# Attention on TensorE in one piece per unit, a shorter bias table, one scalar transfer, and the first query tiles of both batches first

## The chip, the cores and the metric

The kernel runs on one core of a Trainium2 chip. The metric is device time in microseconds (us) of one execution, as the median of several; less is better. PE is TensorE (PEld its weight loads), DVE is VectorE, ACT is ScalarE, POOL is GpSimd, SP is SyncE, which here only issues DMAs.

## The reference, cut to what matters

```
scores = scale * q @ k^T                        # B=2, H=8, S=768, D=64, float32
keep = (pos_k < n_global) | (0 <= rel < n_local)     # 8 global keys, 96 local ones
dist = where(is_global & ~is_local, n_local, abs(rel))
scores = where(keep, scores - slope[h] * dist, -1e9)
a = softmax(scores); attn = a @ v               # as x: 1536 tokens x 512
x = ((x @ w_a) * (x @ w_b)) @ w_out             # d_ff = 1536
out = ((x @ w1) * (x @ w2)) @ w3 @ w_out2       # d_ff = 1024
```

## The kernel before

The work is cut into attention and two gated products stages. A query tile is 128 tokens of one batch (6 tiles for each of 2 batches), and a **unit** is four heads of a query tile: 24 units. A unit sees 232 keys (8 global, 96 before the tile, 128 own); in the first tile of a batch it sees only its own 128, and such a unit is called short. A unit takes these steps: scores (L558, four matmuls into banks 0 and 1), bias and row maximum (L533, DVE, from the table `tabs`), exponential (L537, ACT), sum plus 1e-9 and reciprocal (L579, L580, DVE), scaling (L542, POOL), transposes (L602, into banks 2 and 3), their copies to SBUF (L611 by ACT, L613 by DVE), values (L620, into bank 4), and two parts `xh` (L637, ACT) and `xl` (L638, DVE) of the result, which the products read.

The products are float32 in three float32r matmuls each (L188, L189, L190: high by high, high by low, low by high), 128x512 apiece, over three chunks of 512 tokens; 2352 such product matmuls stand in the program. Their weights come as float64 words in 1 MB transfers (L447) and pass through L455 to L465 on DVE, POOL and ACT (four DVE instructions a piece) into a `slot`. The first chunk needs four query tiles, that is eight units, and the weights `w_a` and `w_b` of group 0.

What order the engines work in is fixed beforehand. The class `Plan` lists operations as strands that each name an engine, a planned duration and the time when they are ready; it always takes the operation that could start first (a lower rank breaks ties), and the program is written in that order for every engine. So a strand's rank, its planned cost and how many operations it hands over together set the order. In `attention` each unit is a strand of its own: two score operations, and in `half(u)` two transposes operations and two values operations, each free to stand between products. A unit may begin when fewer than four are under way. The products are another strand of higher rank, and they fill PE where no attention is ready.

At the start, two DMAs on ACT's queue (L153, L154) bring the two int64 scalars; DVE turns them into floats (L159 to L164), sets a flag for a fallback that these inputs do not take (L175 to L180), and makes the bias table from two iotas in eight instructions (L198 to L201, L420 to L423); ACT and POOL scale it per head (L427, L429). The table's room is in `pT0`, `pT1` and `qk1`, so `qk1` can be loaded only after L427 and L429. SP issues all other DMAs in one queue.

Of the kernel before, what the change touches and what calls it, by code (L numbers as in the profile page):

```python
# [8 lines left out]
F32 = mybir.dt.float32  # L9
# [8 lines left out]
FMAX = 3.0e38  # L18

# [87 lines left out]
def attention_moe_moe_kernel(  # L107
# [4 lines left out]
    n_global: bass.AP,  # L112
    n_local: bass.AP,
# [45 lines left out]
    nc.vector.tensor_copy(wf, words)  # L159
    lo_w = wf.rearrange("p (n w) -> p n w", w=2)[:, :, 0]  # L160
    hi_w = wf.rearrange("p (n w) -> p n w", w=2)[:, :, 1]
    nc.vector.tensor_scalar(neg[:, 0:2], lo_w, 0.0, None, ALU.is_lt)
    nc.vector.tensor_tensor(neg[:, 2:4], neg[:, 0:2], hi_w, ALU.add)
    nc.vector.scalar_tensor_tensor(nval, neg[:, 2:4], 4294967296.0, lo_w, ALU.mult, ALU.add)  # L164
# [3 lines left out]

    ftmp = const.tile([P, 4], F32, tag="ftmp", name="ftmp")
    flag = const.tile([P, 1], I32, tag="flag", name="flag")  # L170

    const.tile([P, 40], F32, tag="gap", name="gap")
    xh = const.tile([P, KD, NT], F32R, tag="xh", name="xh")
    xl = const.tile([P, KD, NT], F32R, tag="xl", name="xl")
    nc.vector.tensor_scalar(ftmp[:, 0:1], ng, float(NG_MAX), None, ALU.is_gt)  # L175
    nc.vector.tensor_scalar(ftmp[:, 1:2], nl, 1.0, None, ALU.is_lt)
    nc.vector.tensor_scalar(ftmp[:, 2:3], nl, float(NPREV + 1), None, ALU.is_gt)
    nc.vector.tensor_tensor(ftmp[:, 3:4], ftmp[:, 0:1], ftmp[:, 1:2], ALU.max)
    nc.vector.tensor_tensor(ftmp[:, 0:1], ftmp[:, 2:3], ftmp[:, 3:4], ALU.max)
    nc.vector.tensor_copy(flag, ftmp[:, 0:1])  # L180
# [199 lines left out]
    D_MM = lambda n: 0.016 + 0.000417 * n  # L380
# [3 lines left out]
    with ExitStack() as fast:  # L384
# [32 lines left out]
        keep = jj  # L417
        masks(loc, keep, rel, jj)

        nc.vector.scalar_tensor_tensor(rel, rel, nl, loc, ALU.subtract, ALU.mult)  # L420
        nc.vector.scalar_tensor_tensor(rel, rel, nl, keep, ALU.add, ALU.mult)
        nc.vector.tensor_scalar(keep, keep, MASKED / slopes[-1], -MASKED / slopes[-1], ALU.mult, ALU.add)
        nc.vector.tensor_tensor(table, keep, rel, ALU.subtract)  # L423

        for h in range(H):
            if h < 5:
                nc.scalar.activation(tabs[:, h, :], table, AF.Copy, scale=8.0 * slopes[h])  # L427
            else:
                nc.gpsimd.tensor_scalar(tabs[:, h, :], table, 8.0 * slopes[h], 1.0, ALU.mult, ALU.mult)  # L429
        T0 = 10.5  # L430
        pl.free |= {"DVE": T0, "ACT": T0 + 2.5, "POOL": T0 + 2.0, "PE": 5.0}
        qkb.free[1] = T0 + 1.0

# [70 lines left out]

        xr = {}
        att = {"began": 0, "done": 0, "end": 0.0}
        obank = Ring([bank[4]])
        tbank = Ring([bank[2], bank[3]])
        sbank = Ring([(bank[0], bank[1])])
        tiles = {}  # L510

        def load(b, t):
            i, r = yield from qkb.get()
            j, r2 = yield from vvb.get()
            x, y = qkb.tiles[i], vvb.tiles[j]
            if t == 0:

                def fn():
                    nc.sync.dma_start(x[:, :, 0:P], qk[b, t, :, :, 0:P])
                    nc.sync.dma_start(x[:, :, P + KB:], qk[b, t, :, :, P + KB:])  # L520
                tq = yield op("DMA", 2.0, r, fn)
                tv = yield op("DMA", 0.9, r2, lambda: nc.sync.dma_start(y[:, 0, :], vv[b, t, :, 0, :]))
            else:
                tq = yield op("DMA", 2.4, r, lambda: nc.sync.dma_start(x, qk[b, t]))
                tv = yield op("DMA", 1.7, r2, lambda: nc.sync.dma_start(y, vv[b, t]))
            tiles[b, t] = i, j, tq + 2.2, tv + 2.2

        def head(rank, st, m, h, sS, ei, s, t, c0, res):

            n = KW - c0  # L530
            e = eb.tiles[ei][:, c0:KW]
            nmx, sm = st[:, m:m + 1], st[:, 4 + m:5 + m]
            a = yield op("DVE", 0.21 + 0.00104 * n, s, lambda: nc.vector.tensor_tensor_reduce(  # L533
                out=e, in0=sS, in1=tabs[:, h, 0:P] if t == 0 else tabs[:, h, P:TW],
                scale=-0.125, scalar=FMAX, op0=ALU.add, op1=ALU.min, accum_out=nmx))
            res["ttr"].append(a + LAT)
            a = yield op("ACT", D_ACT(n) + 0.28, a + LAT, lambda: nc.scalar.activation(  # L537
                e, e, AF.Exp, bias=nmx, scale=-1.0, accum_out=sm))
            res["exp"].append(a + LAT)

        def scaled(e, rs, r, res, u):
            res["e", u].append((yield op("POOL", 0.56, r, lambda: nc.gpsimd.tensor_scalar(  # L542
                e, e, rs, 1.0, ALU.mult, ALU.mult))) + LAT)

        def attention(num, b, t, g):

            yield lambda: 0.0 if att["began"] == num and (b, t) in tiles and num - att["done"] < 4 else None
            i, jv, tq, tv = tiles[b, t]
            x, y = qkb.tiles[i], vvb.tiles[jv]
            c0 = KB if t == 0 else 0  # L550
            sk, r = yield from sbank.get()
            sS = [bk.rearrange("p (u k) -> p u k", u=2)[:, :, 0:KW] for bk in [z[:, 0:2 * KW] for z in sbank.tiles[sk]]]

            def scores(u):
                p = 2 * g + u
                for j in range(2):
                    rr = slice(64 * j, 64 * j + 64)
                    nc.tensor.matmul(sS[j][:, u, c0:KW], x[rr, p, 0:P], x[rr, p, P + c0:P + KW], start=True, stop=True)  # L558

            s = []  # L560
            for u in range(2):
                s.append((yield op("PE", 0.32, max(tq, r), lambda u=u: scores(u))) + PELAT)
            att["began"] += 1
            k, r = yield from stb.get()
            st = stb.tiles[k]
            res = {"ttr": [], "exp": [], ("e", 0): [], ("e", 1): []}
            es = []
            for u in range(2):
                for j in range(2):
                    m = 2 * u + j  # L570
                    ei, r2 = yield from eb.get()
                    es.append(ei)
                    pl.spawn(head(num, st, m, 4 * g + m, sS[j][:, u, c0:KW], ei, max(s[u], r, r2), t, c0, res), 10 + 0.1 * num)
            sbank.free[sk] = yield lambda: max(res["ttr"]) if len(res["ttr"]) == 4 else None
# [402 lines left out]
```

## Time and profile before

| | |
|---|---|
| median of 3 runs | 650.99 us (649.75 to 652.82) |
| the profiled execution | 650.21 us |
| its span, first to last instruction | 648.3 us |
| PE busy in the span | 95% |
| DVE, ACT, POOL busy | 61%, 39%, 17% |
| the two scalar DMAs are issued | at 0.74 and 1.15 us |
| weights A and B of group 0 are issued | at 2.78 and 3.25 us |
| first product starts | at 60.15 us |

A row of the timeline gives start, duration, engine, line and operation; rows that repeat are merged with their count, and a wait ahead of a row stands in brackets with what ended it. PE's matmuls are pipelined: a row's duration overlaps the next one's, so what a matmul takes from the engine is the distance from one start to the next. A wait's releaser is inferred, and an engine that is named may have been done long before.

### The profile page before, as it was taken

Reading aid. Unit: us, or ns where it says so; the run is one execution under the profiler, and the core shown is the slowest. Engines: PE = TensorE matmul, PEld = TensorE weight load, DVE = VectorE, ACT = ScalarE, POOL = GpSimd, SP = SyncE. Lnnn points to the kernel's source line nnn. Section 1 sums busy time; section 2 is a strip of 40 time slices with the busy share of each in tenths; the row PEclk is TensorE's granted clock in tenths of the full one; section 3 lists DMA queues with packets and bytes.
Section 4 is the critical chain, followed back from the end, with each engine's and each line's share of the span. In section 5 each row is a group of like instructions: output and inputs, shape, how many; then the busy total and the mean of one; then the engine's idle time right before and its main releaser. Section 6 shows DMA issues by size and latency. Waiting matters only on the chain.

```text
span 648.3 us, 8069 instructions
## 1 busy us (share of the span) xinstructions
PE 617.2 (95%) x3072; PEld 496.1 (77%) x3072; DVE 394.4 (61%) x694; ACT 250.5 (39%) x486; POOL 108.9 (17%) x149
## 2 busy tenths in 40 slices
PE   1778999999999999999999999999999999999996
PEld 1445777777888888888888888888888888888884
DVE  5789765556366997766878654981376266323333
ACT  3767666554244434324343223542452133111110
POOL 3548423323022111101101100120021010000000
PEclk9989999999999999999999999999999999999999
DMA  7528222340033333303333000420240030000012
GB/s 251 195 104 312 63 79 108 128 163 1 1 130 129 131 129 130 130 1 130 129 131 115 16 0 1 161 99 1 73 174 13 1 130 2 1 0 1 32 66 102
DMA packets 12815, 57.79 MB, mean 89 GB/s; under 512 B 1504, under 2 KB 3552, under 8 KB 7904
## 3 DMA queue, kind: packets, MB, share of 16 engines
q1 hardware_dynamic: 12480, 57.19, 24.8%
q8 instruction: 26, 0.43, 0.3%
q14 instruction: 21, 0.17, 0.1%
q10 hardware_dynamic: 288, 0.00, 0.0%
HBM read 54.04 MB, written 3.15 MB: 88 GB/s over the span
## 4 chain that ended last, share of the span: by engine, by line
PE 93%; DVE 4%; DMA 1%; ACT 1%; issue 1%; POOL 0%; ACTq 0%; POOLq 0%; DVEq 0%; SPq 0%
PE bank L188 28%; PE bank L190 28%; PE bank L189 27%; PE bank L558 3%; PE bank L620 3%; PE bank L602 3%; DMA words<-in_n_local_dram 1%; DVE e L533 1%; DMA qk<-in_qk_dram 1%; DVE raw L460 1%; DVE pT L613 1%; ACT tabs L427 0%; DVE xl L638 0%; DVE acc L705 0%; DVE raw L458 0%
## 5 line engine op out<-in xcount | busy, mean ns | idle before, releaser
L188 PE MATMUL bank<-xh,slot 128*128 128x512 f32 x480 | 190.1, 396 | 0.0
L190 PE MATMUL bank<-xh,slot 128*128 128x512 f32 x480 | 187.0, 390 | 0.0
L189 PE MATMUL bank<-xl,slot 128*128 128x512 f32 x480 | 186.9, 389 | 0.0
L456 POOL TENSOR_SCALAR raw<-raw 128x1024 f32<-128x1024 f32 x38 | 54.0, 1425 | 337.9 <-DMA raw<-in_moe_w_dram 179.6
L705 DVE TENSOR_TENSOR acc<-acc,bank 128x512 f32<-128x512 f32 x96 | 65.7, 684 | 71.5 <-PE bank L190 71.3
L188 PEld LDWEIGHTS bank<-xh,slot 128*128 128x128 f32 x480 | 90.1, 188 | 21.4 <-issue 3.6
L190 PEld LDWEIGHTS bank<-xh,slot 128*128 128x128 f32 x480 | 90.1, 188 | 18.9
L189 PEld LDWEIGHTS bank<-xl,slot 128*128 128x128 f32 x480 | 90.2, 188 | 17.6
L668 ACT ACTIVATE gh<-gt 128x512 fp32r<-128x512 f32 x60 | 37.7, 629 | 112.4 <-DVE gt L664 112.4
L664 DVE TENSOR_TENSOR gt<-gt,bank 128x512 f32<-128x512 f32 x60 | 41.1, 685 | 64.6 <-PE bank L190 64.3
L661 ACT ACTIVATE gt<-bank 128x512 f32<-128x512 f32 x60 | 35.8, 597 | 87.8 <-PE bank L190 87.6
L542 POOL TENSOR_SCALAR e<-e,st 128x232 f32<-128x232 f32 (+1 forms) x96 | 51.6, 556 | 76.8 <-DVE st L580 37.9
L188 PE MATMUL bank<-gh,slot 128*128 128x512 f32 x144 | 56.9, 395 | 0.0
L189 PE MATMUL bank<-gl,slot 128*128 128x512 f32 x144 | 56.1, 390 | 0.0
L190 PE MATMUL bank<-gh,slot 128*128 128x512 f32 x144 | 56.1, 390 | 0.0
L457 ACT ACTIVATE raw<-raw 128x1024 f32<-128x1024 f32 x38 | 43.7, 1153 | 28.8 <-POOL raw L456 28.7
L458 DVE SCALAR_TENSOR_TENSOR raw<-raw 128x1024 int32<-128x1024 int32 x38 | 47.2, 1243 | 10.1 <-ACT raw L457 9.6
L537 ACT ACTIVATE e<-e,st 128x232 f32<-128x232 f32 (+1 forms) x96 | 44.6, 466 | 15.3 <-DVE st L533 14.8
L460 DVE SCALAR_TENSOR_TENSOR raw<-raw 128x1024 int32<-128x1024 int32 x38 | 49.4, 1301 | 0.5
L669 DVE TENSOR_TENSOR gl<-gt,gh 128x512 fp32r<-128x512 f32 x60 | 44.7, 746 | 4.7 <-ACT gh L668 4.5
L558 PE MATMUL bank<-qk 64*128 64x232 f32 (+1 forms) x192 | 27.6, 403 | 16.0 <-DMA qk<-in_qk_dram 10.9
L533 DVE CUSTOM_DVE_ANT_0 e<-bank,tabs 128x232 f32<-128x232 f32 (+1 forms) x96 | 32.7, 375 | 16.3 <-PE bank L558 15.2
(68 smaller groups left out, 735.0 us busy)
## 6 DMA issues: line engine op xcount, KB each, us to landing
raw<-in_moe_w_dram SPq DMA_DIRECT2D x16, 1024.0 KB, 4.8
raw<-in_moe_w_out_dram SPq DMA_DIRECT2D x10, 1024.0 KB, 5.1
qk<-in_qk_dram SPq DMA_DIRECT2D x10, 720.0 KB, 5.1
raw<-in_moe_w_a_dram SPq DMA_DIRECT2D x6, 1024.0 KB, 5.6
raw<-in_moe_w_b_dram SPq DMA_DIRECT2D x6, 1024.0 KB, 6.4
vv<-in_vv_dram SPq DMA_DIRECT2D x10, 512.0 KB, 3.6
out_dram<-acc SPq DMA_DIRECT2D x12, 256.0 KB, 2.0
qk<-in_qk_dram SPq DMA_DIRECT2D x4, 256.0 KB, 5.8
```

The source lines that it names most:

```text
L188: nc.tensor.matmul(po, sh, mh, start=first, stop=False)
L189: nc.tensor.matmul(po, sh, ml, start=False, stop=False)
L190: nc.tensor.matmul(po, sl, mh, start=False, stop=last)
L456: a = yield op("POOL", 1.2, t, lambda: nc.gpsimd.tensor_scalar(tf, tf, F64_MAX, -F64_MAX, ALU.min, ALU.max))
L457: a = yield op("ACT", D_ACT(1024), a + LAT, lambda: nc.scalar.activation(tf, tf, AF.Copy, scale=2.0 ** -112))
L458: c = yield op("DVE", 1.25, max(a, c) + LAT, lambda: nc.vector.scalar_tensor_tensor(low, top, 3, low, ALU.logical_shift_left, ALU.bitwise_or))
L460: t = yield op("DVE", 1.25, c + LAT, lambda: nc.vector.scalar_tensor_tensor(low, top, -0x80000000, low, ALU.bitwise_and, ALU.bitwise_or))
L537: a = yield op("ACT", D_ACT(n) + 0.28, a + LAT, lambda: nc.scalar.activation(e, e, AF.Exp, bias=nmx, scale=-1.0, accum_out=sm))
L542: res["e", u].append((yield op("POOL", 0.56, r, lambda: nc.gpsimd.tensor_scalar(e, e, rs, 1.0, ALU.mult, ALU.mult))) + LAT)
L558: nc.tensor.matmul(sS[j][:, u, c0:KW], x[rr, p, 0:P], x[rr, p, P + c0:P + KW], start=True, stop=True)
L669: a = yield op("DVE", D_DVE(CH), a + LAT, lambda: nc.vector.tensor_tensor(gl, gt, gh.bitcast(F32), ALU.subtract))
L705: u = yield op("DVE", D_DVE(CH), max(t + PELAT, accr[c, m]), lambda: nc.vector.tensor_tensor(a(), a(), po, ALU.add))
```

## The change

It does five things. The two scalars come as one array `n_words` that is laid out for 128 partitions, in one DMA. The table is made in six DVE instructions, three of them ahead of the scalars, in the room of the accumulators instead of `qk1`; five heads' tables are scaled by ACT, three by POOL as before; the flag's instructions become a strand of low rank. The query tiles go in the order (batch 0, batch 1) for tile 0, then for tile 1 and so on, so that the four short units come first; their q and k are loaded by pairs of heads. `load` is split in two strands, for q with k and for v. And PE's attention work becomes one strand: a piece holds the values of unit i-1, the transposes of unit i and the scores of unit i+2; from the ninth on it is one operation that waits for everything it needs. Planned costs of scores, transposes, values and products are changed too. Nothing of the arithmetic of the products changes.

```diff
-    nc.scalar.dma_start(words[:, 0:2], n_global.bitcast(I32).partition_broadcast(P))
-    nc.scalar.dma_start(words[:, 2:4], n_local.bitcast(I32).partition_broadcast(P))
+    nc.scalar.dma_start(words, n_words)
...
-    D_MM = lambda n: 0.016 + 0.000417 * n
+    D_MM = lambda n: 0.227 * n / 512
...
-        rel, jj, loc = [ptb.tiles[i][:, 0:TW] for i in range(2)] + [qkb.tiles[1].rearrange("p a b -> p (a b)")[:, 0:TW]]
-        table = qkb.tiles[1].rearrange("p a b -> p (a b)")[:, TW:2 * TW]
+        rel, relq, jj, near, dist = [a.rearrange("p m f -> p (m f)")[:, i * TW:(i + 1) * TW]
+                                     for a in accs for i in range(4)][:5]
...
-        masks(loc, keep, rel, jj)
-        nc.vector.scalar_tensor_tensor(rel, rel, nl, loc, ALU.subtract, ALU.mult)
-        nc.vector.scalar_tensor_tensor(rel, rel, nl, keep, ALU.add, ALU.mult)
-        nc.vector.tensor_scalar(keep, keep, MASKED / slopes[-1], -MASKED / slopes[-1], ALU.mult, ALU.add)
-        nc.vector.tensor_tensor(table, keep, rel, ALU.subtract)
+        nc.vector.tensor_scalar(near, rel, 0.0, 2.0 ** 20, ALU.is_lt, ALU.mult)
+        nc.vector.tensor_tensor(rel, rel, near, ALU.max)
+        nc.vector.tensor_scalar(relq, rel, 1.0 / FAR, None, ALU.mult)
+        read_words()
+        nc.vector.tensor_scalar(nlq, nl, 1.0 / FAR, None, ALU.mult)
+        nc.vector.scalar_tensor_tensor(near, rel, nl, relq, ALU.is_ge, ALU.add)
+        nc.vector.tensor_scalar(dist, jj, ng, nlq, ALU.is_ge, ALU.add)
+        nc.vector.tensor_tensor(dist, dist, near, ALU.min)
...
+        order = [(b, t) for t in range(NQ) for b in range(B)]
...
+        def load_qk(n, b, t):
...
             if t == 0:
...
+                for g in range(2):
+                    pp = slice(2 * g, 2 * g + 2)
+                    tq = yield op("DMA", 1.0, r, lambda pp=pp: nc.sync.dma_start(x[:, pp, KB:KB + 2 * P], qk[b, t, :, pp, KB:KB + 2 * P]))
...
+        def scores(num):
...
+            for u in range(2):
+                for j in range(2):
+                    rr = slice(64 * j, 64 * j + 64)
+                    nc.tensor.matmul(sS[j][:, u, 0:w], x[rr, 2 * g + u, KW:KW + P], x[rr, 2 * g + u, KW - w:KW], start=True, stop=True)
+        def transposes(num):
...
+            for m in range(4):
+                for c, (k0, _) in enumerate(blocks):
+                    i = (m % 2) * nb + c
+                    nc.tensor.transpose(pts[m // 2][:, i * P:(i + 1) * P], eb.tiles[ev["e", num][1][m]][:, k0:k0 + P], ident)
...
+            def part(what, num):
...
+                if what == "S":
+                    def r():
+                        if ("q", num) not in ev or (num and ("ttr", num - 1) not in ev):
+                            return None
...
+                    return r, 0.3 + 0.34 * nb, lambda: scores(num), then
...
+                    return r, 0.1 + 0.87 * nb, lambda: transposes(num), then
...
+                return r, 0.2 + 0.54 * nb, lambda: values(num), then
+            for i in range(-2, NU + 1):
+                ps = [part(w, n) for w, n in (("V", i - 1), ("T", i), ("S", i + 2)) if 0 <= n < NU]
+                whole = i > 8
+                for k in range(1 if whole else len(ps)):
+                    now = ps if whole else ps[k:k + 1]
...
+                    t = yield op("PE", sum(x[1] for x in now), t, fn)
...
-            for g in range(2):
-                pl.spawn(attention(2 * n + g, b, t, g), 8 + 0.1 * n)
+        pl.spawn(attention(), 8)
```

How the instructions move, at three places. **PE where attention stands among the products** (`bank_97` and `bank_98` before, `bank_87` and `bank_88` now, are product banks). Before:

```order
L188 MATMUL bank_97<-xh,slot_100 128x512
L189 MATMUL bank_97<-xl,slot_100 128x512
L190 MATMUL bank_97<-xh,slot_100 128x512
L602 MATMUL bank_94<-ident,e_128 128x128 x2
L602 MATMUL bank_94<-ident,e_129 128x128 x2
L558 MATMUL bank_92<-qk_124 128x232
L558 MATMUL bank_93<-qk_124 128x232
...
L620 MATMUL bank_96<-pT_141,vv_125 64x128 x4
L188 MATMUL bank_98<-xh,slot_100 128x512
```

and now:

```order
L194 MATMUL bank_88<-xh,slot_90 128x512
L641 MATMUL bank_86<-pT_130,vv_115 64x128 x4
L641 MATMUL bank_86<-pT_131,vv_115 64x128 x4
L630 MATMUL bank_84<-ident,e_118 128x128 x2
L630 MATMUL bank_84<-ident,e_119 128x128 x2
L630 MATMUL bank_85<-ident,e_120 128x128 x2
L630 MATMUL bank_85<-ident,e_121 128x128 x2
L622 MATMUL bank_82<-qk_114 128x232
L622 MATMUL bank_83<-qk_114 128x232
...
L192 MATMUL bank_88<-xh,slot_90 128x512
```

From the first product to the last attention instruction, attention stood in 39 groups with products between them, and now it stands in 16. Before the first product there were the scores of 10 units, the transposes of 9 and the values of 8 and a half (two of the units short); now the scores of 11, the transposes of 9 and the values of 8 (four short). The stretch with products held the scores of 14 units, the transposes of 15, the values of 15.5 (two of the units short) and 210 product matmuls; now it holds the scores of 13, the transposes of 15, the values of 16 (all full) and 171 product matmuls.

**DVE at the start.** Before (`wf` to `nval` are the scalars, `pT_140`, `pT_141` and `qk_124` hold the table):

```order
L159 CAST wf<-words 128x4
...
L164 SCALAR_TENSOR_TENSOR nval<-neg,wf 128x2
L175 TENSOR_SCALAR ftmp<-nval 128x1
...
L180 CAST flag<-ftmp 128x1
L198 TENSOR_SCALAR qk_124<-pT_140,nval 128x360
...
L423 TENSOR_TENSOR qk_124<-pT_141,pT_140 128x360
L533 ISA e_128,st_116<-bank_92,tabs 128x128
```

and now (`acc_92` and `acc_93` hold it):

```order
L424 TENSOR_SCALAR acc_92<-acc_92 128x360
L425 TENSOR_TENSOR acc_92<-acc_92 128x360
L427 TENSOR_SCALAR acc_92<-acc_92 128x360
L170 CAST wf<-words 128x4
...
L175 SCALAR_TENSOR_TENSOR nval<-neg,wf 128x2
L429 TENSOR_SCALAR nlq<-nval 128x1
L431 SCALAR_TENSOR_TENSOR acc_92<-acc_92,nval 128x360
L432 TENSOR_SCALAR acc_93<-acc_92,nval,nlq 128x360
L433 TENSOR_TENSOR acc_93<-acc_93,acc_92 128x360
L554 ISA e_118,st_106<-bank_82,tabs 128x128
```

Eight wide instructions and the flag's six stood between the scalars and the first reduction; now three wide ones and a small one do. The flag's six stand in the row after the scores of unit 7.

**SP at the start.** Before:

```order
L519 DMA qk_123<-in_qk_dram 128x4x128
L520 DMA qk_123<-in_qk_dram 128x4x128
L522 DMA vv_125<-in_vv_dram 128x512
L447 DMA raw_114<-in_moe_w_a_dram 128x2048
L447 DMA raw_115<-in_moe_w_b_dram 128x2048
L447 DMA raw_142<-in_moe_w_out_dram 128x2048
L836 TENSOR_LOAD flag
L524 DMA qk_124<-in_qk_dram 128x1440
```

and now:

```order
L529 DMA qk_113<-in_qk_dram 128x2x256 x2
L539 DMA vv_115<-in_vv_dram 128x512
L529 DMA qk_114<-in_qk_dram 128x2x256 x2
L539 DMA vv_116<-in_vv_dram 128x512
L455 DMA raw_104<-in_moe_w_a_dram 128x2048
L455 DMA raw_105<-in_moe_w_b_dram 128x2048
L532 DMA qk_113<-in_qk_dram 128x1440
L455 DMA raw_132<-in_moe_w_out_dram 128x2048
```

Both short tiles, 0.75 MB each with their values, now stand ahead of the weights; the load of the flag stands behind 21 DMAs instead of 6.

## Rows read from the trace of the kernel before

**Rows 1.** Busy time of PE by stretch: from, to, length, PE busy, granted clock, DMA share, GB/s.
```profile
0.00:60.10 60.10, 35.46 (x264) 0.97 0.60 224
60.10:155.50 95.40, 95.40 (x669) 1.00 0.27 97
```

**Rows 2.** Timeline, 0 to 21 us: start, us, engine, line, operation, shapes.
```profile
6.67 0.17 DVE L159 CAST wf<-words 128x4 f32<-128x4 int32 x1 [6.67 <-DMA words<-in_n_local_dram]
...
8.11 0.15 DVE L180 CAST flag<-ftmp 128x1 int32<-128x1 f32 x1
...
11.58 0.53 DVE L423 TENSOR_TENSOR qk<-pT,pT 128x360 f32<-128x360 f32 x1
...
12.68 0.29 DVE L533 CUSTOM_DVE_ANT_0 e<-bank,tabs 128x128 f32<-128x128 f32 x1 [0.57 <-ACT tabs L427]
...
14.29 0.33 SPq L524 DMA_DIRECT2D qk<-in_qk_dram  x1
...
18.55 1.92 PE L558 MATMUL bank<-qk 64*128 64x232 f32 x8 [3.11 <-DMA qk<-in_qk_dram]
```

**Rows 3.** DMA issues, 0 to 20 us: queue, count, KB each, us from issue to landing.
```profile
raw<-in_moe_w_a_dram SPq DMA_DIRECT2D x1, 1024.0 KB, 8.1
raw<-in_moe_w_b_dram SPq DMA_DIRECT2D x1, 1024.0 KB, 10.1
...
words<-in_n_global_dram ACTq DMA_DIRECT2D x1, 1.0 KB, 2.7
```

**Rows 4.** Busy time of all engines by stretch from 12.6 us; before the last numbers the clock.
```profile
50.00:60.15 10.15, 7.35 (x75) 5.10 (x71) 8.76 (x28) 7.76 (x25) 7.34 (x11) 1.00 0.99 394
sum 47.55, PE 34.28 PEld 22.75 DVE 40.13 ACT 35.24 POOL 28.34; mean PE 6.86 PEld 4.55 DVE 8.03 ACT 7.05 POOL 5.67
```

**Rows 5.** Groups of DVE instructions, 12.6 to 60.15 us: busy us, mean ns, idle before.
```profile
L533 DVE CUSTOM_DVE_ANT_0 e<-bank,tabs 128x232 f32<-128x232 f32 x32 | 11.5, 392 | 3.6 <-PE bank L558 3.5
L455 DVE TENSOR_SCALAR raw<-raw 128x1024 int32<-128x1024 int32 x5 | 6.3, 1288 | 0.0
...
L638 DVE TENSOR_TENSOR xl<-bank,xh 128x256 fp32r<-128x256 f32 x8 | 3.4, 420 | 1.0 <-ACT xh L637 1.0
...
L533 DVE CUSTOM_DVE_ANT_0 e<-bank,tabs 128x128 f32<-128x128 f32 x8 | 2.1, 286 | 0.9 <-ACT tabs L427 0.6
```

**Rows 6.** Timeline of PE from 105.85 us: scores and transposes between two products.
```profile
105.85 0.40 PE L189 MATMUL bank<-xl,slot 128*128 128x512 f32 x1
106.08 0.40 PE L190 MATMUL bank<-xh,slot 128*128 128x512 f32 x1
106.41 1.05 PE L558 MATMUL bank<-qk 64*128 64x232 f32 x8
107.39 1.09 PE L602 MATMUL bank<-ident,e 128*128 128x128 f32 x8
108.24 0.48 PE L188 MATMUL bank<-gh,slot 128*128 128x512 f32 x1
108.56 0.40 PE L189 MATMUL bank<-gl,slot 128*128 128x512 f32 x1
```

**Rows 7.** Timeline of PE from 109.8 us: values, then transposes.
```profile
109.81 1.10 PE L620 MATMUL bank<-pT,vv 104*64 104x128 f32 x16
110.84 1.09 PE L602 MATMUL bank<-ident,e 128*128 128x128 f32 x8
```

**Rows 8.** Busy time of all engines in single microseconds; before the last two numbers the clock.
```profile
38.00:39.00 1.00, 0.00 (x0) 0.00 (x0) 1.00 (x2) 1.00 (x3) 1.00 (x1) 1.00 0.98 382
41.00:42.00 1.00, 1.00 (x8) 0.41 (x4) 0.95 (x1) 0.00 (x0) 1.00 (x1) 0.52 0.04 17
```

**Rows 9.** Timeline of PE, 40 to 45 us: a unit's scores, values and transposes.
```profile
40.57 1.50 PE L558 MATMUL bank<-qk 64*128 64x232 f32 x8
42.01 1.12 PE L620 MATMUL bank<-pT,vv 104*64 104x128 f32 x8
43.05 1.75 PE L602 MATMUL bank<-ident,e 128*128 128x128 f32 x8
```

More of the change, by code (lines that the diff above doesn't have):

```diff
@@ L158, in attention_moe_moe_kernel @@
     nval = const.tile([P, 2], F32, tag="nval", name="nval")
[L159 to L164, printed above, removed]
+    nlq = const.tile([P, 1], F32, tag="nlq", name="nlq")
@@ L502, in prep_group @@
                               (tag, st, g), gate), rank)
+        order = [(b, t) for t in range(NQ) for b in range(B)]
+        NU = 2 * len(order)
         xr = {}
         att = {"began": 0, "done": 0, "end": 0.0}
[L507 to L512, printed above, removed]
+        sS = [[bk[:, 0:2 * KW].rearrange("p (u k) -> p u k", u=2) for bk in bank[0:2]]][0]
+        pts = bank[2:4]
+        po = bank[4][:, 0:2 * P].rearrange("p (u k) -> p u k", u=2)
@@ L543, in scaled, with softmax @@
                 e, e, rs, 1.0, ALU.mult, ALU.mult))) + LAT)
[L545 to L563, printed above, removed]
+        def softmax(num, s):
@@ L564, in attention @@
             k, r = yield from stb.get()
             st = stb.tiles[k]
-            res = {"ttr": [], "exp": [], ("e", 0): [], ("e", 1): []}
+            res = {"ttr": [], "exp": [], "e": []}
             es = []
[L568 to L573, printed above, removed]
@@ L610, in half, with evicted @@
+            ev["e", num] = (yield lambda: max(res["e"]) if len(res["e"]) == 4 else None), es, k
+        def evicted(num, t):
+            _, blocks = width(num)
+            w = 2 * len(blocks) * P
+            r = []
+            for u, eng in ((0, "ACT"), (1, "DVE")):
+                pT, pt = ptb.tiles[u], pts[u]
                 if u == 0:
-                    a = yield op("ACT", D_ACT(w), max(a + PELAT, r2), lambda: nc.scalar.activation(pT[:, 0:w], pt[:, 0:w], AF.Copy))
+                    fn = lambda pT=pT, pt=pt: nc.scalar.activation(pT[:, 0:w], pt[:, 0:w], AF.Copy)
@@ new lines, in transposes, with values @@
+        def transposes(num):
+            _, blocks = width(num)
+            nb = len(blocks)
+            for m in range(4):
+                for c, (k0, _) in enumerate(blocks):
+                    i = (m % 2) * nb + c
+                    nc.tensor.transpose(pts[m // 2][:, i * P:(i + 1) * P], eb.tiles[ev["e", num][1][m]][:, k0:k0 + P], ident)
+        def values(num):
+            n, g = divmod(num, 2)
+            y = vvb.tiles[ev["v", num][0]]
+            _, blocks = width(num)
+            nb = len(blocks)
+            for u in range(2):
+                for c, (_, nk) in enumerate(blocks):
+                    for j in range(2):
+                        h, i = 4 * g + 2 * u + j, j * nb + c
+                        nc.tensor.matmul(po[64 * j:64 * j + 64, u, :], y[0:nk, nb - 1 - c, h * D:(h + 1) * D],
+                                         ptb.tiles[u][0:nk, i * P:(i + 1) * P], start=(c == 0), stop=(c == nb - 1))
@@ L786, in switch @@
         def switch():
-            yield lambda: 0.0 if att["done"] == 2 * B * NQ else None
+            yield lambda: 0.0 if att["done"] == NU else None
             t = att["end"]
-            gbank.add(list(sbank.tiles[0]), t)
-            ybank.add(list(tbank.tiles), t)
+            gbank.add(bank[0:2], t)
+            ybank.add(bank[2:4], t)
             r = yield lambda: raw.free[2]
@@ L939, in _laid_out @@
     r = dict(inputs)
-    r["qk"] = _np.concatenate([by_pair(q, own), by_pair(k, keys)], 4)
+    n = _np.array([inputs["n_global"], inputs["n_local"]], dtype=_np.int64).view(_np.int32)
+    r["n_words"] = _np.tile(n, (P, 1))
+    r["qk"] = _np.concatenate([by_pair(k, keys), by_pair(q, own)], 4)
     pad = _np.concatenate([prev, _np.zeros((NQ, P - prev.shape[1]), prev.dtype)], 1)
```

200 lines of the change are left out of this document (112 added, 88 removed).

## The prediction

> **What bounds the kernel now.** Read the busy time by stretch first: from the first product at 60.1 us to the end of attention PE is busy 95.40 of 95.40 us, while before that it works only 35.46 of 60.10 us [rows 1]. So two things set the end: when the first product starts, and how much PE work stands behind it. In the second stretch a wait of another engine costs nothing and every gap of PE's own costs in full; in the first, PE waits.
>
> The timeline of the start shows for what. DVE gets the scalars at 6.67 us, works on flag and table until 12.11 us, and makes the first reduction at 12.68 us. The load of the second tile is issued at 14.29 us, when its room stops being the table's, and the third unit's scores start at 18.55 us behind it [rows 2]. From the first reduction to the first product DVE is busy 40.13 of 47.55 us, more than ACT (35.24) or POOL (28.34) [rows 4]: DVE, with the waits between it and PE, sets the pace there.
>
> **The change, part by part.** I sum against the profiled execution: its own time is 650.21 us, its span 648.30, and 0.8 us lie between its time and the median of 650.99, which I add at the end.
>
> *Scalars and table.* The ten small instructions take 6.67 to 8.26 us, 0.16 each; the eight wide ones take 3.85 us, 0.48 each; from the table to the first reduction it is 0.57 us [rows 2]. After the change five small (0.8) and three wide ones (1.45) and the 0.57 stand behind the scalars: 2.8 us instead of 6.0. Three wide ones lie ahead of the scalars, where DVE has nothing to do. The one transfer is issued at 0.74 us as the first of the two was; the first landed 2.7 us after its issue [rows 3], the second just before 6.67 us [rows 2]. So the first reduction comes at 6.2 to 9.5 us by the table if the first unit's scores are there, whose tile is loaded in the same microseconds. I take the later landing, since one transfer now carries what the pair did, beside the same loads, and a little off it for the earlier issue: 9.2 us instead of 12.68.
>
> *DVE's work up to the first product.* The four short units first mean that of the 40 reductions in this stretch 24 are 232 wide and 16 are 128 wide, instead of 32 and 8: 8 x (0.392 - 0.286) = 0.8 us less. One weight instruction fewer stands there (four L455 of 1.288, not five): 1.3 less. One `xl` fewer: 0.4 less [rows 5]. The flag's six come in: 0.9 more. So 40.1 becomes 38.5 us. Idle of DVE was 7.4 us [rows 4]; of that the 0.6 for the tables and about half of the 3.5 for scores [rows 5] belong to the late table and the late second tile, and go. 5.1 us remain. Ends for this: 1 us, if the earlier loads feed every step, and 9, if the pieces hold each other up, since now the transposes of a unit and the scores two units on stand in one row. Then the scores of the eleventh unit (1.0) and the first product: 9.2 + 38.5 + 5.1 + 1.0 = 53.8 us, against 60.15: **6.35 us earlier** (ends 49.7 and 57.7).
>
> *The queues.* SP now loads 1.5 MB of tiles ahead of the weights instead of 0.75. Weights A and B landed 8.1 and 10.1 us after issue [rows 3], at 10.9 and 13.4 us; 0.75 MB at 394 GB/s [rows 4] is 1.9 us. DVE's shift of B stands ahead of the third unit's reductions, and POOL's clamp of A ahead of the first unit's scaling, so at worst DVE idles 2 us there; I count that inside the 5.1. The load of the flag is no longer ahead of the second tile, and stands behind a reload that waits for a later DVE instruction, so it costs nothing. The reload of `w_out` waits for the last weight instruction before the products, and a tile's values and q and k queue behind it: 1.0 + 0.5 + 0.7 MB, 5.7 us at that rate. Their scores stand two pieces and 33 product matmuls later, over 10 us; if that cover were gone it would be some 3 us, once.
>
> *PE's work behind the first product.* The product matmuls are the same 2352. A full unit costs, by starts: scores 106.41 to 107.39, 0.98; transposes 107.39 to 108.24, 0.85 [rows 6]; values 109.81 to 110.84, 1.03 [rows 7]. Between two products the distance is 0.23; into attention it is 0.33 and behind it 0.32 [rows 6], so each group of attention costs 0.10 + 0.09, say 0.2 us more. Before, 39 groups held 12 full and 2 short units' scores, 13 and 2 transposes, 13.5 and 2 values; with short ones at half (scores two thirds) that is 13.1 + 11.9 + 14.9 + 7.8 = 47.7 us, and 95.4 - 210 x 0.229 = 47.3 is what the stretch shows [rows 1]. Now 16 groups hold 13, 15 and 16 full ones: 12.7 + 12.8 + 16.5 + 3.2 = 45.2. The merging saves 4.6 us, and 2.1 of it goes into work that used to be done ahead of the first product: **2.5 us less**.
>
> *A new wait.* In this stretch a piece is one operation in PE's order: if the copies for the values, the scaling for the transposes or the reductions for the scores are late, everything on PE behind it stands, the products too. Before, the stretch showed none [rows 1]. A piece and the nine to twelve product matmuls behind it last 5.1 to 5.8 us; DVE has some 3 us of attention in that and a little for the products, and while group 1's weights are made (four pieces, with more product matmuls between them) another 3 to 4. Ends: nothing, and 10 us, if in those four pieces two weight instructions of 1.3 us each lie in front. I take 2, near the lower end, since most pieces leave DVE a third of the time free. Here a rule speaks against the change: the Trainium skill ("Perfetto Trace Analysis", Matmuls) asks that independent matmul groups rotate through PSUM banks, so that the evacuation of one overlaps the next; values keep their single bank here and scores their single pair. By it the waits would be a pattern at every piece, which is the second rival.
>
> Sum: 650.21 - 6.35 - 2.5 + 2.0 = 643.4; with the 0.8 to the median, **644.2 us**.
>
> **The rivals.**
>
> 1. *DVE never starves.* Idle 1 us instead of 5.1, and no waits at the pieces: 650.21 - 10.4 - 2.5 + 0.8 = 638.1. For it: both short tiles are loaded before the weights. Against it: ACT and POOL share the same steps, and 7.4 us of idle stood there before.
>
> 2. *The merged pieces wait, each a little.* At each of the 16 pieces PE stands for the last of three inputs. From 0.35 us a piece on, the gain is under 0.5%; at 0.7, half of one weight instruction, it is 11.2 instead of 2: 652.6, no change. For it: one order for three inputs, where before a unit's halves could slip past each other between products. Against it: scores have two pieces' time to come back as transposes.
>
> 3. *The lower clock holds through the start.* After a stretch in which PE did nothing (38 to 39 us) the granted clock was 0.52, that is 1.2 GHz for most of the microsecond from 41 us [rows 8]. At it a full unit's scores took 1.44, half its values 1.04 and its transposes 1.75 [rows 9]: 5.3 us for a piece instead of 2.9. Short pieces leave PE idle between them, and if the five full pieces before the first product all run so, that is 12 us: first product at 65.8, 650.21 + 5.65 - 2.5 + 2 + 0.8 = 656.2, slower. It decides when more than half of the pieces before the first product run at 1.2 GHz. Against it: slower pieces fill PE's idle time, and only some 4 us ran so before. The Trainium skill ("TensorE: Matmul & The Clock Gate", HAM oscillation) says that idle gaps between bursts throw the array back to the lower clock; rows 8 agree once, and whether the new gaps are long enough no row shows.
>
> That the change does not do what it says is excluded for PE: the order has 16 groups.
>
> **How the numbers follow.** A change of 0.5%, 3.3 us, is about what a measurement of this kernel can tell from none. Forecast 0.60 (own range 640 to 649, a twentieth of it above 647.7), rival 1 0.12, rival 2 0.19 (a fifth of it still faster, a tenth slower), rival 3 0.09 (a third of it within 0.5%). Faster: 0.57 + 0.12 + 0.04 = 0.73; within: 0.03 + 0.13 + 0.03 = 0.19; slower: 0.02 + 0.06 = 0.08. The range, 638.5 to 652, leaves out rival 3, about a third of rival 2 and half of rival 1.
>
> **What would show it.** First reduction near 9 us; scores of the third unit well before 18 us; first product near 54; from there to the end of attention PE busy throughout but for some 2 us, with 16 groups of attention, 45 us in all, among 171 product matmuls; then the same 490 us as before. Wrong it would be if the first product came at 57 or later, if PE's list of waits showed several us behind DVE or POOL after it, or if the granted clock were near 0.5 for many microseconds before it.

## The result, and the profile after

The changed kernel takes **645.88 us** (median of 8 runs, 642.65 to 646.98) against 651.01 (649.75 to 653.69): ratio 0.9913, interval 0.9893 to 0.9933. Forecast were 644.2 us and a gain of over 0.5%. The profiled execution took 646.13 us with a span of 644.2.

Busy time of PE by stretch: start, mixed stretch to the end of attention, rest (columns as in [rows 1]).

```profile
0.00:55.63 55.63, 35.03 (x241) 0.91 0.65 239
55.63:142.54 86.91, 86.91 (x653) 1.00 0.33 109
142.54:644.20 501.66, 495.20 (x2183) 1.00 0.20 70
```

The first product comes 4.52 us earlier than before (at 60.15 us). The mixed stretch holds 171 product matmuls; 86.91 - 171 x 0.229 leaves 47.7 us for attention, where before it was 47.3. The rest holds the products that are left: 39 more than before, which is why it lasts 501.7 us and not the 490 of the prediction; per product it is the same. So 650.21 - 4.5 + 0.4 = 646.1: all that was won was won ahead of the first product, and more was expected there.

The timeline of the start (columns as in [rows 2]):

```profile
3.42 0.16 DVE L170 CAST wf<-words 128x4 f32<-128x4 int32 x1
...
5.27 0.53 DVE L433 TENSOR_TENSOR acc<-acc,acc 128x360 f32<-128x360 f32 x1
...
6.37 0.29 DVE L554 CUSTOM_DVE_ANT_0 e<-bank,tabs 128x128 f32<-128x128 f32 x1 [0.57 <-ACT tabs L438]
```

The scalars are used at 3.42 us instead of 6.67 [rows 2], and the first reduction stands at 6.37 instead of 12.68. Of these 6.3 us only 4.5 reach the first product. Busy time of all engines from the first reduction to it (columns as in [rows 4]), and what DVE waited for in the same stretch (total us, times, longest):

```profile
6.37:55.63 49.26, 33.80 (x233) 22.92 (x233) 40.49 (x138) 34.30 (x109) 26.96 (x45) 0.90 0.65 245
```

```profile
DVE raw L463 <- DMA raw<-in_moe_w_a_dram: 3.5, 2, 2.1
DVE e L554 <- PE bank L622: 1.8, 2, 1.1
DVE pT L599 <- PE bank L630: 1.1, 1, 1.1
DVE e L554 <- POOL e L563: 1.1, 1, 1.1
...
```

DVE idles 8.8 us, not 5.1. The longest wait is for a weight that nobody needs yet. The timeline shows it: SP issues weight A of group 1 at 39.89 us, and DVE's first instruction on it stands ahead of DVE's copy for the eighth unit's values.

```profile
39.89 0.42 SPq L455 DMA_DIRECT2D raw<-in_moe_w_a_dram  x1
...
48.33 0.70 DVE L463 TENSOR_SCALAR raw<-raw 128x1024 int32<-128x1024 int32 x1 [2.11 <-DMA raw<-in_moe_w_a_dram]
...
48.94 1.05 DVE L580 TENSOR_SCALAR st<-st 128x4 f32<-128x4 f32 x1
...
50.12 0.66 DVE L599 COPY pT<-bank 128x512 f32<-128x512 f32 x1
```

(The small L580 behind that weight instruction takes 1.05 us; at 42.38 us it took 0.16. POOL's L464 works on the same weight from 48.38 to 49.96 us; whether that is the reason was not tested.)

On PE's timeline the second half of those values waits for the copy, and what follows takes twice its usual time:

```profile
46.62 0.66 PE L641 MATMUL bank<-pT,vv 104*64 104x128 f32 x8 [0.34 <-ACT pT L597]
50.83 1.12 PE L641 MATMUL bank<-pT,vv 104*64 104x128 f32 x8 [3.55 <-DVE pT L599]
51.88 1.97 PE L630 MATMUL bank<-ident,e 128*128 128x128 f32 x8
53.78 1.92 PE L622 MATMUL bank<-qk 64*128 64x232 f32 x8
55.63 0.79 PE L192 MATMUL bank<-xh,slot 128*128 128x512 f32 x1
```

The windows of single microseconds show the clock; the granted clock (third number from the end) is 1.00 until PE has stood idle from 47.3 us on, and then goes to 0.50, the 1.2 GHz level:

```profile
47.00:48.00 1.00, 0.28 (x6) 0.03 (x2) 0.00 (x0) 0.00 (x0) 0.00 (x0) 1.00 1.05 442
48.00:49.00 1.00, 0.00 (x0) 0.00 (x0) 0.67 (x2) 0.00 (x0) 0.62 (x1) 1.00 0.95 401
49.00:50.00 1.00, 0.00 (x0) 0.00 (x0) 0.99 (x2) 0.00 (x1) 0.96 (x1) 0.74 0.98 410
50.00:51.00 1.00, 0.17 (x2) 0.17 (x4) 0.98 (x3) 1.00 (x1) 0.61 (x2) 0.50 1.05 434
```

One more list, PE's waits ahead of the first product, became the key to the rest. Transposes (L630) wait for POOL's scaling, and in PE's order the scores two units on stand behind them:

```profile
PE bank L630 <- POOL e L563: 9.9, 6, 4.7
PE bank L641 <- DVE pT L599: 4.1, 2, 3.6
PE bank L622 <- DMA qk<-in_qk_dram: 3.8, 1, 3.8
PE bank L622 <- DVE st L554: 2.1, 1, 2.1
...
```

Last, the mixed stretch: the distance from a unit's transposes to its neighbour's scores is 1.02 us (67.98 to 69.00). To a product it was 0.85 [rows 6].

```profile
66.94 1.10 PE L641 MATMUL bank<-pT,vv 104*64 104x128 f32 x16
67.98 1.09 PE L630 MATMUL bank<-ident,e 128*128 128x128 f32 x8
69.00 1.05 PE L622 MATMUL bank<-qk 64*128 64x232 f32 x8
69.98 0.50 PE L192 MATMUL bank<-xh,slot 128*128 128x512 f32 x1
```

### The profile page after: what moved, and what is told of

Read it like the earlier page. It is cut to its first block, busy times and chain, and to the rows that moved or that the text cites. A ratio compares the mean times of both kernels' runs of the same rounds, so it can differ in the third digit from the quotient of the medians.

```text
span 644.2 us, 8087 instructions
## 1 busy us (share of the span) xinstructions
PE 617.1 (96%) x3072; PEld 499.5 (78%) x3072; DVE 396.0 (61%) x693; ACT 249.9 (39%) x486; POOL 105.0 (16%) x149
## 4 chain that ended last, share of the span: by engine, by line
PE 92%; DVE 3%; DMA 2%; POOL 1%; issue 1%; SPq 0%; ACT 0%; ACTq 0%
PE bank L192 28%; PE bank L194 28%; PE bank L193 28%; PE bank L630 3%; PE bank L641 3%; PE bank L622 2%; DMA raw<-in_moe_w_a_dram 2%; POOL e L563 1%; DVE e L554 1%; DVE st L580 1%; DVE raw L463 0%; SPq L529 0%; DVE slot L473 0%; DVE pT L599 0%; DVE acc L765 0%
## 5 line engine op out<-in xcount | busy, mean ns | idle before, releaser
L464 POOL TENSOR_SCALAR raw<-raw 128x1024 f32<-128x1024 f32 x38 | 52.5, 1381 | 355.6 <-DMA raw<-in_moe_w_dram 157.4
L563 POOL TENSOR_SCALAR e<-e,st 128x232 f32<-128x232 f32 (+1 forms) x96 | 49.2, 531 | 65.3 <-DVE st L581 28.1
L466 DVE SCALAR_TENSOR_TENSOR raw<-raw 128x1024 int32<-128x1024 int32 x38 | 47.8, 1259 | 9.2 <-ACT raw L465 8.8
L468 DVE SCALAR_TENSOR_TENSOR raw<-raw 128x1024 int32<-128x1024 int32 x38 | 48.5, 1275 | 0.4
L472 ACT ACTIVATE slot<-raw 128x1024 fp32r<-128x1024 f32 x26 | 29.5, 1134 | 33.6 <-PE bank L193 23.8
L473 DVE TENSOR_TENSOR slot<-raw,slot 128x1024 fp32r<-128x1024 f32 x26 | 32.7, 1257 | 14.4 <-ACT slot L472 14.2
```

The costliest lines, as they stand in the source:

```text
L464: a = yield op("POOL", 1.2, t, lambda: nc.gpsimd.tensor_scalar(tf, tf, F64_MAX, -F64_MAX, ALU.min, ALU.max))
L466: c = yield op("DVE", 1.25, max(a, c) + LAT, lambda: nc.vector.scalar_tensor_tensor(low, top, 3, low, ALU.logical_shift_left, ALU.bitwise_or))
L468: t = yield op("DVE", 1.25, c + LAT, lambda: nc.vector.scalar_tensor_tensor(low, top, -0x80000000, low, ALU.bitwise_and, ALU.bitwise_or))
L563: res["e"].append((yield op("POOL", 0.3 + 0.0011 * e.shape[1], r, lambda: nc.gpsimd.tensor_scalar(e, e, rs, 1.0, ALU.mult, ALU.mult))) + LAT)
```

## The experiments

The theory: the start sets the gain; in the changed kernel the wait for weight A, the lower clock behind it and later the order within a piece give part of it back. The rivals: the merged pieces are the gain, the start being hidden; or the loads only trade places. All times are medians of 4 to 8 runs. The ratios to the kernel before have intervals of 0.15 to 0.27% to either side, so medians some 3 us apart differ beyond doubt; single executions of one kernel lie up to 5.3 us apart.

| kernel | us | first product | attention behind it |
|---|---|---|---|
| changed | 645.9 | 55.6 | 47.7 |
| e1 old table | 645.8 | 55.0 | 47.4 |
| e2 one strand per unit | 643.3 | 49.6 | 51.2 |
| e3 batch by batch | 641.9 | 56.1 | 45.4 |
| e4 weights requested early | 642.2 | 52.5 | 47.4 |
| e5 PE filled | 646.0 | 55.1 | 48.5 |
| e6 e4, old table | 645.4 | 53.9 | 47.4 |
| e7 e4, batch by batch | 639.6 | 50.4 | 45.1 |
| e8 e4, scores before transposes | 637.6 | 48.3 | 46.7 |
| e9 scores before transposes | 637.4 | 47.5 | 46.7 |
| e10 e2, batch by batch | 644.6 | 50.4 | 51.1 |
| e11 e8, batch by batch | 636.3 | 49.7 | 44.1 |
| e12 e9, old table | 640.3 | 51.5 | 46.5 |

The two columns on the right are of the profiled execution; the last is the mixed stretch less 0.229 us for each product matmul in it.

**The change undone part by part: e1, e2, e3.** In e1 the eight wide instructions stand behind the scalars again:

```diff
+        masks(loc, keep, rel, jj)
+        nc.vector.scalar_tensor_tensor(rel, rel, nl, loc, ALU.subtract, ALU.mult)
...
-        nc.vector.scalar_tensor_tensor(near, rel, nl, relq, ALU.is_ge, ALU.add)
-        nc.vector.tensor_scalar(dist, jj, ng, nlq, ALU.is_ge, ALU.add)
-        nc.vector.tensor_tensor(dist, dist, near, ALU.min)
```

> The changed kernel with the old table: eight wide DVE instructions behind the scalars instead of three, the flag's six ahead of them, and the scalars in two transfers; the table stays in the room of the accumulators. Theory (the start sets the gain): the first reduction falls back from 6.4 to about 12.5 us, and of these 6 us some 2 are taken up by waits that DVE has anyway (raw A lands at 11 us), so the first product comes at 59 to 61 us instead of 55.6 and the time is 649 to 652. Rival (the merged pieces are the gain, the start is hidden behind the weights' loads): the first product moves by less than 2 us and the time is 645 to 648.

A miss: the numbers are the rival's. The first reduction fell back to 12.04 us as expected, yet the first product came no later and the time stayed. DVE's work on group 1's weight A now stood behind the eighth unit's copy, so the wait of 3.55 us and the lower clock at that place were gone (an earlier stretch at the lower clock, 6.8 us of it from 34 to 42 us, stood in this execution). From the first reduction to the first product, columns as in [rows 4]:

```profile
12.04:55.01 42.97, 33.24 (x232) 22.28 (x232) 35.34 (x128) 31.87 (x107) 26.07 (x44) 0.92 0.57 207
```

DVE works 5.2 us less there than in the changed kernel and idles 1.1 us less: one each of the weight instructions L466 and L468 of the changed kernel has gone behind the first product, and the flag's six ahead of the first reduction. In this kernel, then, the table buys nothing: the 5.7 us by which it brings the first reduction forward go into the weight work that the order puts ahead of the first product, and its wait. That the start is hidden, the rival's reason, does not hold in the better orders of e6 and e12 below.

In e2 attention's strands are as before (`attention(num)` with `half(u)`, which also brings back their planned costs), the rest as changed. Its last lines:

```diff
-        pl.spawn(attention(), 8)
+        for num in range(NU):
+            pl.spawn(attention(num), 8 + 0.1 * num)
```

> The changed kernel with attention on PE as before: one strand per unit, scores, transposes and values in halves that stand freely between products (39 groups between products instead of 16). Theory (the merging does not pay on PE, since transposes followed by scores take 1.02 us instead of 0.85): PE's attention time behind the first product stays within 1 us of 47.7 for the same number of units, the first product comes within 2 us of 55.6, and the time is 644 to 648. Rival (merging is the gain): 649 or more.

A miss in all three points, and the rival fell too: the time, 643.3 us in the median and 643.7 at most, lies below the theory's range, and the first product came 6 us earlier. PE's attention behind it is 51.2 us, but with the scores of 14 units and the transposes of 16 instead of 13 and 15, in 39 groups. For the same units (0.98 + 0.85 less) it is 49.4, so one piece per unit does save 1.7 us on PE. Ahead of the first product it costs 6.1 us, of which 1.8 are PE's work on the unit that now stands behind it: 4.3 us by that count. DVE's row shows in what form:

```profile
6.38:49.57 43.19, 32.15 (x217) 22.21 (x217) 34.54 (x121) 29.81 (x97) 22.05 (x38) 0.88 0.61 233
```

DVE idles 8.7 us, as in the changed kernel, but does 34.5 us of work before the first product instead of 40.5; one unit's reductions and one each of the weight instructions L463, L466 and L468 are no longer among it. The medians are 2.6 us apart, at the edge of what the runs can tell.

In e3 only the order of tiles goes back:

```diff
-        order = [(b, t) for t in range(NQ) for b in range(B)]
+        order = [(b, t) for b in range(B) for t in range(NQ)]
```

> The changed kernel with the query tiles batch by batch, so that two short units stand at the start and two later. Theory (short tiles first saves DVE 0.8 us ahead of the first product, and a smaller second load): the first product 1 to 2 us later, the time 646 to 648, and two short units' worth of PE work (about 3 us) leaves the stretch ahead of nothing, so no more. Rival (the early second short tile is what lets the start flow): the scores of the third unit wait for a 1.4 MB tile beside the weights, the first product comes 4 us later or more, the time is 649 to 652.

Both fell: it is 4.0 us faster. The first product comes only 0.4 us later, while the two short units left behind it cut PE's work there by 2.3 us. The profiled execution took 644.8 us, the longest of its five, so it can't show where the other 1 to 2 us of the median come from. The stretch where PE never waits is the one that gains by the cheap units, here.

**The wait for weight A: e4, e5.**

```diff
-    GP = 8
+    GP = 5
```

> The changed kernel with one number changed: the weights of group 1 may be requested after 5 begun units instead of 8, which puts the load of weight A on SP's queue ahead of the sixth tile while the DVE order stays nearly the same. Theory (DVE stood 2.1 us in its queue for that load, PE 3.5 us behind DVE, and the lower clock followed from PE's idle time): both waits go, the granted clock stays near 1 from 48 us on, the first product comes at 51.5 to 53.5 us, and the time is 642 to 644. Rival (the loads only trade places): the tile behind the weight lands late instead, PE waits for its scores, and the first product stays at 55 to 56.5, the time within 1 us of 645.9.

As the theory had it: 52.51 us and 642.2. The weight is issued at 23.08 us instead of 39.89, DVE's wait for it is gone (1.1 us is left, that of group 0), and the clock stays at 2.4 GHz at this place (an earlier stretch, 31 to 39 us, ran at 1.2 GHz for 6.8 us):

```profile
48.00:49.00 1.00, 0.53 (x8) 1.00 0.96 115
49.00:50.00 1.00, 0.22 (x4) 1.00 0.57 238
50.00:51.00 1.00, 1.00 (x14) 1.00 1.06 451
51.00:52.00 1.00, 1.00 (x9) 1.00 0.97 395
```

(PE alone: length, busy, clock, DMA share, GB/s.) The first product's 3.1 us are 1.6 us less work of DVE and 1.5 less idle time. To separate the clock from the wait, e5 leaves the wait and gives PE something to do in it:

```diff
+                        if num == 7 and u == 1 and c == 0 and j == 0:
+                            for _ in range(32):
+                                nc.tensor.transpose(bank[5][:, 0:P], ident, ident)
```

> The changed kernel with 32 transposes of the identity put into PE's order between the two halves of the eighth unit's values, where PE stood 3.55 us for DVE; their results go to a bank that the first product overwrites. At 0.106 us each they fill 3.4 us of a wait that stays. Theory (the clock fell because PE stood idle): DVE still waits 2 us for weight A, but the granted clock stays near 1 from 48 to 57 us, the transposes and scores behind the wait take 1.02 and 0.98 us instead of 1.9 each, the first product comes at 53.5 to 54.2 us and the time is 1.5 to 2 us less, 643.8 to 644.4. Rival (the clock falls there for another reason): it is near 0.5 as before, the first product at 55.5 or later, the time 645.5 to 646.5.

Its timeline of PE at that place:

```profile
48.88 3.71 PE L643 MATMUL bank<-ident 128*128 128x128 f32 x32
52.52 0.66 PE L644 MATMUL bank<-pT,vv 104*64 104x128 f32 x8
53.11 1.11 PE L630 MATMUL bank<-ident,e 128*128 128x128 f32 x8
54.15 1.05 PE L622 MATMUL bank<-qk 64*128 64x232 f32 x8
55.14 0.50 PE L192 MATMUL bank<-xh,slot 128*128 128x512 f32 x1
```

and the clock there (columns as in e4):

```profile
49.00:50.00 1.00, 1.00 (x10) 1.00 0.99 418
50.00:51.00 1.00, 1.00 (x11) 1.00 1.04 434
```

On the clock the theory held: 1.00 in every microsecond from 48 to 56 us, and from the second half of the values to the first product 2.62 us instead of 4.80. On the time it missed: 646.0, in the rival's range, and the first product at 55.1. This execution had run at the lower clock for some 10 us between 25 and 40 us, where that of the changed kernel had 3.4 (a microsecond at clock c counted as (1 - c) / 0.5), and reached the place 1.7 us later; and attention behind the first product took 0.8 more, 0.5 of it waits of PE. What the lower clock alone costs in a median stays open; that PE's idle time brings it at this place is shown, in one execution of each kernel. Not every gap does: in the changed kernel PE stood idle from 8.7 to 13.5 us too, and the clock stayed at 1.00.

**The table again: e6.** e4 and the old table, so that no wait for weight A stands in either.

> The kernel of e4 (weights of group 1 requested after 5 units) with the old table and the scalars in two transfers. No wait for weight A stands in either, so the two differ by the table alone. Theory (a late first reduction is half taken up by DVE's waits for raw A and raw B at 11 and 13 us): first product 55 to 56 us, 2.5 to 3.5 us behind e4, the time 644.7 to 646. Rival 1 (the whole 5.7 us come through): 58 us and 648. Rival 2 (the table is worth nothing): within 0.7 us of e4's 52.5 and 642.2.

The time is in the theory's range, 3.2 us behind e4; the first product, 53.9 us, is earlier than its 55 to 56. The profiled execution had the clock at 1.00 up to the first product and was the fastest of its six runs, so its 53.9 us may stand low.

**Batch order again: e7.**

> The kernel of e4 with the tiles batch by batch. Theory (short tiles first moves 2.4 us of PE work behind the first product and gives DVE 0.8 us ahead of it): the first product 0.5 to 1.5 us later than e4's 52.5, the stretch with products 2.4 us shorter for the same products, the time 640.3 to 641.7. Rival (the second short tile's early load counts more): first product at 55 or later and 643 or more.

639.6 us, 2.6 less than e4 and below the theory's range. Attention behind the first product fell by 2.3 us as expected; the first product came earlier instead of later, in an execution without any low clock up to there, the fastest of its six.

**The order within a piece: e8, e9.** The last lead of the profile, scores behind waiting transposes:

```diff
-                ps = [part(w, n) for w, n in (("V", i - 1), ("T", i), ("S", i + 2)) if 0 <= n < NU]
+                ps = [part(w, n) for w, n in (("V", i - 1), ("S", i + 2), ("T", i)) if 0 <= n < NU]
```

> The kernel of e4 with the order within a piece values, scores, transposes instead of values, transposes, scores. The planner then puts 117 product matmuls among the pieces instead of 162. Theory (transposes take 1.02 us ahead of scores and 0.85 ahead of a product): attention behind the first product takes 2.2 us less for the same units, 45.3 us, without new waits; first product within 1 us of 52.5; the time 639.5 to 641. Rival (pieces closer together wait for DVE or POOL): PE's list of waits shows several us behind the first product, and the time is 642 or more.

> The changed kernel with nothing but the order within a piece changed: values, scores, transposes. The request for group 1's weights stays after 8 begun units. Theory (in PE's fixed order the scores two units on, which are ready, stood behind transposes that wait for POOL, so DVE was fed late; it was 9.9 us of such waits ahead of the first product): the waits for POOL ahead of the first product fall to 3 to 5 us, the first product comes at 48.5 to 52 us, with some DVE wait for weight A left, and the time is 638 to 642. Rival (e8 owed its gain to the early weights together with this order): first product at 53 or later, 643 or more.

Both are below the theory's ranges: 637.6 with the early weights and **637.4** without, so the order alone does it, 8.5 us less than the changed kernel. In e9 PE's waits for POOL ahead of the first product fall from 9.9 to 2.7 us:

```profile
PE bank L641 <- ACT pT L597: 3.8, 5, 1.2
PE bank L622 <- DMA qk<-in_qk_dram: 3.6, 1, 3.6
PE bank L622 <- DVE st L554: 3.3, 3, 2.4
PE bank L630 <- POOL e L563: 2.7, 2, 2.4
...
```

and DVE, fed earlier, idles 5.0 of 41.11 us; 4.4 us less of its work stand ahead of the first product, among them two weight instructions and a copy:

```profile
6.38:47.49 41.11, 29.96 (x233) 21.26 (x233) 36.07 (x126) 33.02 (x107) 23.83 (x43) 0.96 0.73 262
```

Behind it the transposes stand ahead of a product and take 0.85 us:

```profile
105.24 1.05 PE L622 MATMUL bank<-qk 64*128 64x232 f32 x8
106.22 1.09 PE L630 MATMUL bank<-ident,e 128*128 128x128 f32 x8
107.07 0.48 PE L192 MATMUL bank<-xh,slot 128*128 128x512 f32 x1
```

Attention there takes 46.7 us instead of 47.7, 0.75 of it new waits: the 16 pieces are closer together, with 117 products in the stretch instead of 171. Against e2's strands (643.3 us) one piece per unit in this order is 5.9 us faster: in this order merging pays, and with transposes ahead of scores the order took it back.

**What the parts are worth together: e10, e11, e12.**

> The kernel of e2 (one strand per unit) with the tiles batch by batch: the kernel before with only the new table, the one scalar transfer and the tables' and tiles' new rooms. Theory (of the change's parts only the start pays): first product 50 to 53 us, the stretch behind it with two short units in it, the time 639 to 643, less than the changed kernel's 645.9. Rival (short tiles first and one piece per unit pay in their own right): 646 or more.

> The changed kernel with three edits: weights of group 1 after 5 units, batch by batch, values - scores - transposes. Theory (e7 gave 2.6 us over e4 by units moved back to short, e8 4.6 by the order): if both add up, first product 47 to 49 us, two short units behind it, the time 634.5 to 636.5. Rival (the start is bound by DVE's work, which batch order makes 0.8 us longer, and weights A and B land no earlier): the gain of the batch order shrinks to the 2 us behind the first product less 1 to 2 us ahead of it, 636.5 to 638.

> The kernel of e9 (values, scores, transposes) with the old table and the scalars in two transfers. Theory (the table's gain was there all along, and in the changed kernel the waits behind it took it): with the better order the first reduction's delay from 6.4 to 12.0 us reaches the first product in good part, 50.5 to 53 us against e9's 47.5, and the time is 640 to 643. Rival (DVE waits for raw A and raw B take the delay up): first product within 1.5 us of 47.5, the time 637 to 639.

e10, the kernel before with the new start (and the change's split loads and planned costs of products), takes 644.6 us: a little above the theory's range, below the rival's, and no worse than the whole change. Against e2, batch order gains nothing here: 644.6 instead of 643.3, with 0.8 us more of PE's waits behind the first product. e11 gives 636.3 us, the lowest median of all (ratio to the kernel before 0.9784, interval 0.9768 to 0.98), though 1.1 us below e9 is less than these medians can tell. The time is just inside the theory's range, the first product (49.7) outside it; batch order saves 2.6 us behind the first product and costs 1.4 ahead of it against e8. That is the size that the rival had, but not its reason: DVE's work is 36.3 us in e11 and 36.1 in e8, and it is a wait of DVE for POOL, 3.6 us, that is new. e12 shows what the table is worth once nothing takes it back: 51.5 against 47.5 us, 2.9 us of time.

## Why the prediction was right, step by step

- **The first reduction** was mis-sized: 9.2 us forecast, 6.37 measured. The single transfer landed 2.3 us after its issue; I had taken the later landing of the pair. The path behind it was right, 2.95 us for 2.8.
- **DVE's work to the first product** came to 40.5 us, not 38.5. Reductions saved 1.4 (0.8 forecast), but four each of the weight instructions L466 and L468 stand there where three did, 2.3 us that I had not counted, and the `xl` stayed eight. L463 took 0.72 us instead of 1.29 and so saved 3.4 (1.3 forecast); the small L580 behind it gave 1.9 of that back.
- **DVE's idle time** is the step that failed: 8.8 us for 5.1, near the end of 9 that the prediction gave for pieces that hold each other up. I had priced the raw weights of group 0 at 2 us at worst and looked for group 1's only behind the first product. Their load was issued 8.4 us before it landed, and DVE's order put the first instruction on it ahead of a copy that PE needed. e4 shows the price of that: 3.7 us of the median. The order within the piece is the other part: in e9, with scores ahead of transposes, DVE idles 5.0 us, which is the forecast, and also does 4.4 us less ahead of the first product.
- **The scores of the eleventh unit** took 1.85 us, not 1.0, at the lower clock; in the measured times they lie inside the two terms above.
- Together: 6.37 + 40.5 + 8.8, first product 55.63 for 53.8, the earlier start and the longer middle against each other, which is luck too.
- **PE's work behind it**: 45.2 us forecast, 47.7 measured. The 0.85 us for transposes held ahead of a product; ahead of scores they take 1.02, and 13 times 0.17 are 2.2 of the 2.5 us. e9, with transposes ahead of products, agrees: 46.7 us, 46.0 without its waits.
- **New waits at the pieces**: 2.0 forecast, none measured: the list of waits of the mixed stretch is empty. That the two last errors cancel (47.2 forecast, 47.7 measured) is luck.
- **Rival 1** (DVE never starves) fell with the 8.8 us. **Rival 2** fell too: none of the 16 pieces waits. The rule of the Trainium skill that stood beside it ("Perfetto Trace Analysis", Matmuls: rotate banks) is not borne out in this stretch. That a piece and its products gave the single banks time to be emptied is likely and was not tested; in e9, with fewer products between the pieces, 0.75 us of waits appear. (The prediction's 652.6 us for this rival lacks the 0.8 us to the median that its other sums have; it would be 653.4, still no change.) **Rival 3** came in part: some 10 us at 1.2 GHz, counted as in e5, instead of 3.4, in two stretches. The second stands behind the wait of 3.55 us; ahead of the first, which began at 32 us, PE was busy for 0.36 to 0.82 of each microsecond from 29 us on. The rule of the Trainium skill beside it ("TensorE: Matmul & The Clock Gate", HAM oscillation) agrees with the second, and with e5. Which gaps bring the clock down these traces do not settle, as said at e5.
- That **merging would pay** was right for PE (1.7 us by e2) and wrong in sum for the order chosen: with transposes ahead of scores it costs 4.3 us of the start by e2, and with scores ahead it pays (e9). The rival with the right mechanism, one order for inputs that come at different times, was priced behind the first product, and stood ahead of it, where the prediction had it only as an end of DVE's idle time.

## What to carry to other kernels

In an order that is fixed beforehand, put what is ready ahead of what will wait: scores that feed the pacing engine belong ahead of transposes that wait for a slower one, and a load that is only wanted later must be requested so early, or used so late, that its wait stands in front of nothing. Before crediting a shorter start, follow the time gained to the next wait that could take it. Try cheap units where the engine that sets the pace never waits: that gained 4.0 us in e3 and 2.6 in e7, but not with free strands (e10).

## What was not expected of the hardware

Transposes (float32, 128x128, eight in a row) take 0.85 us of PE ahead of a product matmul and 1.02 ahead of scores on 64 rows; the profile gives them the same 1.09 us of duration in both places, and only the distance of starts tells. Why is not shown. Executions of the same kernel lie up to 5.3 us apart (e3), and the clock at the start explains that only in part: e6's profiled execution had no low stretch ahead of the first product and was the fastest of its runs, e3's had three and was the slowest of its, but e10's had none and was the second slowest of six. A load of 1 MB took from 4.7 us (weight B of group 1 in e7) over 10.4 us (the same weight in the changed kernel, right behind A) to 13.5 us (`w_out` of group 0 in e10).
